# A gated mix of segment attention and a GeGLU block on one core: first loads in 128 KB pieces over two queues, gate and up weights by column halves, a new order

## The chip, the cores and the metric

The kernel runs on one core of a Trainium2 chip. The metric is the device time of one execution in microseconds; the time before is the median of three runs, and one further execution was profiled. Where a time has a place ("at 17.94"), it is counted from the start of the profiled span.

## The reference

With x of 2048 rows by 512 columns (bfloat16), the output is `g * a + (1 - g) * b`, a row at a time, with `g = sigmoid(sum(x * gate_w))`.

- `a` is attention with 32 heads of width 16 in four segments of 512 rows. In each segment: `q = x @ wq`, `k = x @ wk`, `v = x @ wv`; causal softmax attention inside the segment; plus a read of a running memory, `num = phi(q) @ M` over `den = phi(q) . z`, mixed in by a per-head sigmoid of `beta`; then `M` and `z` are increased by `phi(k)^T v` and by the sum of `phi(k)`. `phi(t)` is `t + 1` for positive t and `exp(t)` otherwise. The heads' result goes through `wo`.
- `b = (gelu(x @ w_gate) * (x @ w_up)) @ w_down` with 1792 hidden columns.

## The kernel before

The work is cut into tasks, each a short run of instructions on one engine, numbered by segment s (0 to 3) and a tile index. The task names are used throughout:

- `xtr0`, `xev0`: segment 0's x is loaded row-wise (tile `pt`), transposed on TensorE into `psX`, and copied to `xT` (lines 770 to 779). The digits are the half of the rows and the pair of 128-column blocks. For segments 1 to 3, four transposing DMAs per segment, `ld_x1_0` to `ld_x3_3` (line 343), bring `xT` directly.
- `K`, `Q`, `V`: projections. A K or Q tile is four matmuls of 128x512 (line 443) into one of four PSUM banks; K of segment 0 is made in three parts a, b, c of 256 columns (line 469), where a needs blocks 2 and 3 of the first half of x, b blocks 0 and 1, and c the second half. `Kev`, `Qev`, `Vev` copy the result out on ScalarE or VectorE, and `kpada`, `kpadb` spread K for the score matmuls. A V task is four matmuls of 128x256 or 257 (line 492).
- `st`, `exp`, `msk`, `pv`: score fills into the 2048-column `psX` (line 596), one ScalarE exponential of 1.88 us each (line 602), the causal mask on GpSimd (line 608), and the product with V (line 638). `tp`, `pvp`, `ot` normalise and transpose on VectorE.
- `phk`, `phq`, `mz`, `nd`: phi of k and q, memory write and memory read. `ktr`, `otr`, `vsh` are their DMAs on SyncE's queue (SP).
- `G`, `U`: 14 gate tiles and 14 up tiles per segment, four matmuls each (line 443); `Gev` and `gelu`, `gd` finish the gate, `h` multiplies. `out`, `wo`, `wev`, `oev`, `dma` are the down projection, the output projection, the mix, and the store.
- `warm1`: matmuls on a zero tile at the start (line 377). `betab`, `bexp`, `gq`, `gfull`, `gwtr`, `gwev` prepare the head gates and the row gate.

Nothing is planned while the kernel is built: the string `ORDER` lists every task by name, and the tasks go out on their engines in that order. A suffix after a colon is a bank number for a TensorE task that opens a bank (`G0_1:0`) or the engine for an eviction (`Gev0_1:d` on VectorE, `:a` on ScalarE). Each engine runs its tasks strictly in its order, and the waits between engines follow from what the tasks read and write. Tasks named `ld_` are DMA issues on SP or ScalarE; one with a `wait` list is held on its queue until the named loads have landed, and all that stands behind it on that queue is held too. Before the change, SP issues x0_0, wk0, wq0 (waits for x0_0), wq1 (waits for x0_1), gw, wv (waits for wk0), two transposes of x1 (the first waits for wq0), wg0 (waits for wq1), the two other transposes, beta, wg1 (waits for wv), and after the first `vsh` the weights wu, wo, wd and x2. ScalarE issues wk1 and x0_1.

Of the kernel before, what the change touches and what calls it, by code (L numbers as in the profile page):

```python
# [246 lines left out]
def _build(es, nc, A_x, A_wq, A_wk, A_wv, A_wo, A_beta, B_w_gate, B_w_up, B_w_down, gate_w, out):  # L247
# [216 lines left out]
    def project(s):  # L464
        b, b3 = s % 2, s % R_XT
        k0 = [Slot() for _ in range(4)]
        for nm, kbs, h in (("a", (2, 3), 0), ("b", (0, 1), 0), ("c", (0, 1, 2, 3), 1)) if s == 0 else ():
            for t in range(4):
                one(f"K0_{t}{nm}", PE, len(kbs) * T_MM / 2, [I(lambda e, t=t, i=i, h=h: e.matmul(
                    BK[k0[t].i][:, 256 * h:256 * h + 256], wk[:, i, t * 128:(t + 1) * 128], xT[0][:, i, 256 * h:256 * h + 256],  # L470
                    start=(i == 2 - 2 * h), stop=(i == 1 + 2 * h)), [("xT", 0, i, "h0"), ("wk", i // 2),
                    *([("xT", 0, i)] if h else [])], [bk(k0[t])]) for i in kbs], opens=(nm == "a"))
# [374 lines left out]
warm0 causal1 ld_wk1 ident ld_x0_0 causal0 warm1:0 xtr0_01 consts masks vones0 gwz ld_wk0 ld_x0_1 ld_wq0 xtr0_00  # L847
xev0_01:d K0_2a:1 K0_0a:2 ld_wq1 ld_gw K0_1a:3 xev0_00:d K0_2b xtr0_10 xtr0_11 K0_0b K0_3a:0 K0_3b K0_1b xev0_10:a
xev0_11:d K0_1c Kev0_1:a K0_3c K0_0c K0_2c Kev0_3:a Kev0_0:a Kev0_2:d ld_wv Q0_0:3 Q0_1:0 Qev0_0:a kpadb0_0 kpada0_0
st0_0A gwtr:2 exp0_0A Q0_3:1 kpada0_3 gwev Qev0_1:d V0_3b:3 V0_0b:2 V0_2b:0 Vev0_3b:d ld_x1_0 ld_x1_1 ld_wg0 ld_x1_3  # L850
ld_x1_2 V0_0a:3 Vev0_0b:d Qev0_3:d Vev0_2b:a st0_0B Vev0_0a:a exp0_0B ld_beta ld_wg1 Q0_2:2 V0_2a:0 V0_1a:1 Q1_3:3
Vev0_2a:a Qev0_2:d Qev1_3:d Vev0_1a:a st0_0C kpadb0_3 phka0_0 kpadb0_1 causal kpada0_1 Q1_1:2 Qev1_1:d G0_1:0 V0_3a:1
V0_1b:3 exp0_0C phkb0_0 Vev0_3a:d Gev0_1:d phkc0_0 st0_0D exp0_0D Q1_2:2 G0_2:1 G1_0:0 st0_0E Qev1_2:d Gev1_0:d
kpadb0_2 Vev0_1b:a exp0_0E G0_6:2 G0_0:3 V1_1a:0 betab Gev0_2:d bexp phka0_2 phqa1_2 Gev0_6:d Gev0_0:d vsh0_00 vsh0_01
vsh0_20 vsh0_21 ld_wu1 ktr0_0 ld_wo st0_1A ld_wu0 ld_x2_2 ld_x2_0 ktr0_1 ld_wd0 V1_3a:1 G1_3:2 G0_3:3 msk0_0A msk0_0B
msk0_0C msk0_0D msk0_0E Vev1_3a:d Gev1_3:d Gev0_3:d exp0_1A phkb0_2 Vev1_1a:a st0_1B pv0_0:12 Q1_0:3 G1_2:0 gq tp0_d01
exp0_1B st0_1C exp0_1C Qev1_0:a phkc0_2 tp0_d00 Gev1_2:d K1_0:2 msk0_1B V1_3b:1 K1_1:0 Vev1_3b:d kpada0_2 st0_1D
exp0_1D Kev1_1:d Kev1_0:d pvp0_00 pvp0_01 V1_2a:1 G1_5:3 K1_2:0 Kev1_2:d Gev1_5:a Vev1_2a:d st0_2A G0_5:2 K1_3:3
exp0_2A G0_4:0 Gev0_5:d Gev0_4:d msk0_1C msk0_1A msk0_1D Kev1_3:d kpada1_0 ktr0_2 ktr0_3 pv0_1:12 st0_2B tp0_d11
kpada1_1 tp0_d10 G0_12:0 V1_2b:3 G0_7:2 Vev1_2b:d G0_11:1 G0_8:3 gelu0 gd0_12 gd0_7 G0_10:0 gd0_8 gd0_11 gd0_10  # L860
ld_x2_3 ld_x2_1 G0_13:2 gd0_13 phka1_0 ot0_0 G0_9:3 ld_wd1 G1_1:1 V1_1b:0 mz0_2:2 gd0_9 exp0_2B kpadb1_2 pvp0_10
V1_0b:3 Vev1_1b:d Vev1_0b:d mzacc0_2 U0_5:0 h0_5 mz0_0:3 U0_10:2 st0_2C mzacc0_0 kpadb1_1 h0_10 phka1_2 Gev1_1:d
phkb1_0 G1_6:0 U0_4:3 V1_0a:2 phqa1_0 Vev1_0a:d kpadb1_0 gz0 Gev1_6:d h0_4 exp0_2C st0_2D exp0_2D K2_0:1 G1_4:2 Q2_1:0
Gev1_4:a phkc1_0 Kev2_0:d st0_2E Q2_0:3 U0_13:2 U0_3:1 exp0_2E msk0_2A msk0_2B msk0_2D msk0_2C msk0_2E Qev2_1:d h0_3
h0_13 st0_3A U0_9:0 U0_2:1 K2_1:2 Qev2_0:a phqb1_2 pvp0_11 h0_2 kpada1_2 Kev2_1:d h0_9 exp0_3A st0_3B pv0_2:31 phqb1_0
gr0 exp0_3B U0_7:2 U0_12:0 st0_3C tp0_d21 gz1 ot0_1 tp0_d20 h0_7 go0 U0_11:1 U0_1:3 h0_12 h0_1 kpada2_1 h0_11 U0_6:2
# [76 lines left out]
```

## Time and profile before

| what | value |
|---|---|
| median of three runs | 271.32 us (270.82 to 271.83) |
| profiled execution | 270.53 us |
| its span in the profile | 268.8 us |
| TensorE matmul busy | 257.1 us (96%) |
| VectorE, ScalarE, GpSimd busy | 206.9, 203.0, 95.5 us |
| moved by DMA | 16.48 MB, mean 61 GB/s |
| granted TensorE clock | 1.00 throughout |

A row of TensorE's instructions in order of time gives start, duration, engine (PE, or PEld for the weight load that overlaps), line, operation, tiles, shape and count, and in brackets the idle time before it with what ended it. A matmul's duration contains its pipeline, so a run of four 128x512 matmuls that lasts 1.03 us by its row keeps the engine for four spacings of 0.216, some 0.865 us. The chain that ended last is followed back from the last instruction; each row is a start, a duration, and what the time was spent in. The time between the span and the execution (1.73 us) lies outside the profile.

### The profile page before, as it was taken

The numbers are of one execution on the slowest core, as the hardware profiler recorded it, in microseconds if no ns is written. First come the engines' busy times: TensorE is split into PE (matmuls) and PEld (weight loads), VectorE is DVE, ScalarE is ACT, GpSimd is POOL, SyncE is SP. The second block draws the span as 40 slices with busy tenths as digits, with TensorE's granted clock in tenths as the row PEclk, the third lists the DMA queues.
The fourth block names the chain that finished last, engine by engine and source line by source line (L and its number), as shares of the span: only waits on it lengthen the run. The fifth ranks groups of instructions, "written<-read, shape, count | busy, mean of one in ns | idle before, by whom it ended". The sixth has DMA issues, their size and how long they took to land.

```text
span 268.8 us, 6340 instructions
## 1 busy us (share of the span) xinstructions
PE 257.1 (96%) x2632; PEld 121.4 (45%) x2669; DVE 206.9 (77%) x434; ACT 203.0 (76%) x171; POOL 95.5 (36%) x150
## 2 busy tenths in 40 slices
PE   7989799999999999999999999899999999999995
PEld 4644345543444444444454444445443444444342
DVE  1458898397989707898588998997899659887883
ACT  1668779889689987899878787777788886868712
POOL 6008271027333502442125464145513034254500
PEclk9999999999999999999999999999999999999999
DMA  6881799600000253002063000012301000012012
GB/s 195 246 226 22 188 246 196 176 2 2 2 2 0 57 104 81 1 2 59 0 100 83 0 2 2 0 43 62 61 2 40 0 2 2 0 48 63 12 41 78
DMA packets 30117, 16.48 MB, mean 61 GB/s; under 512 B 20488, under 2 KB 29064, under 8 KB 30088
## 3 DMA queue, kind: packets, MB, share of 16 engines
q1 hardware_dynamic: 29544, 15.55, 24.6%
q10 hardware_dynamic: 544, 0.52, 0.6%
q8 instruction: 21, 0.34, 0.5%
q14 instruction: 8, 0.07, 0.1%
HBM read 8.14 MB, written 2.10 MB: 38 GB/s over the span
## 4 chain that ended last, share of the span: by engine, by line
PE 74%; DVE 12%; DMA 4%; issue 3%; SPq 2%; ACT 2%; POOL 1%; ACTq 0%; DVEq 0%
PE psD L443 38%; PE psD L715 16%; PE psX L596 7%; PE psD L638 4%; PE psD L729 4%; PE psD L492 3%; DMA xT<-in_A_x_dram 2%; DVE gb L700 2%; DMA pt<-in_A_x_dram 2%; SPq L343 1%; POOL pt L608 1%; ACT pt L602 1%; PE psD L540 1%; PE psD L571 1%; DVE kD L481 1%
## 5 line engine op out<-in xcount | busy, mean ns | idle before, releaser
L602 ACT ACTIVATE pt<-psX 128x2048 bf16<-128x2048 f32 x72 | 135.1, 1877 | 39.8 <-PE psX L596 38.0
L608 POOL TENSOR_TENSOR pt<-pt,ctri 128x256 bf16<-128x256 bf16 x128 | 91.5, 721 | 158.6 <-ACT pt L602 139.3
L443 PE MATMUL psD<-xT,wu 128*128 128x512 bf16 x213 | 52.7, 380 | 1.3 <-issue 0.5
L715 PE MATMUL psD<-wd,gb 128*128 128x512 bf16 x217 | 52.8, 380 | 0.9 <-issue 0.6
L443 PE MATMUL psD<-xT,wg 128*128 128x512 bf16 x213 | 51.4, 379 | 2.3 <-DVE gb L437 1.3
L700 DVE TENSOR_TENSOR gb<-psD,gb 128x512 bf16<-128x512 f32 x56 | 37.6, 683 | 9.7 <-PE psD L443 9.5
L443 PEld LDWEIGHTS psD<-xT,wg 128*128 128x128 bf16 x224 | 20.9, 98 | 26.3 <-DVE gb L437 1.5
L715 PEld LDWEIGHTS psD<-wd,gb 128*128 128x128 bf16 x224 | 20.2, 98 | 24.7 <-issue 3.4
L443 PEld LDWEIGHTS psD<-xT,wu 128*128 128x128 bf16 x224 | 20.0, 97 | 23.5 <-issue 2.6
L596 PE MATMUL psX<-qT,kD 32*128 32x192 bf16 (+7 forms) x512 | 28.6, 287 | 0.3 <-DVE kD L481 0.2
L523 DVE STREAM_TRANSPOSE tT<-psD 128x512 f32<-128x512 f32 x32 | 22.0, 703 | 5.1 <-PE psD L638 4.8
L499 DVE CAST vnat<-psD 128x256 bf16<-128x256 f32 x20 | 8.4, 419 | 14.8 <-PE psD L492 14.6
L638 PE MATMUL psD<-pt,vnat 64*17 64x128 bf16 (+7 forms) x512 | 18.9, 283 | 0.1
L492 PE MATMUL psD<-wv,xT 128*128 128x256 bf16 (+1 forms) x128 | 18.5, 273 | 0.5 <-DVE omem L554 0.5
L649 DVE SCALAR_TENSOR_TENSOR ob<-tT,gq,rc 128x256 bf16<-128x256 f32 x32 | 17.7, 552 | 1.1
L638 PE MATMUL psD<-pt,vsh 64*17 64x128 bf16 (+7 forms) x512 | 18.4, 283 | 0.0
L596 PEld LDWEIGHTS psX<-qT,kD 32*128 32x128 bf16 x512 | 8.2, 92 | 22.3 <-issue 7.8
L683 ACT ACTIVATE gb<-psD 128x512 bf16<-128x512 f32 x28 | 15.2, 593 | 3.9 <-PE psD L443 3.9
L437 DVE CAST gb<-psD 128x512 bf16<-128x512 f32 x23 | 15.6, 682 | 2.3 <-PE psD L443 2.3
L443 PE MATMUL psD<-xT,wq 128*128 128x512 bf16 x61 | 15.8, 380 | 1.2 <-DMA xT<-in_A_x_dram 1.0
L729 PE MATMUL psD<-wo,oT 128*128 128x512 bf16 (+1 forms) x65 | 15.5, 366 | 0.4 <-issue 0.3
L492 PEld LDWEIGHTS psD<-wv,xT 128*128 128x128 bf16 x128 | 12.0, 97 | 7.8 <-DVE omem L554 1.0
(83 smaller groups left out, 268.1 us busy)
## 6 DMA issues: line engine op xcount, KB each, us to landing
out_dram<-ost SPq DMA_DIRECT2D x15, 128.0 KB, 1.7
wg<-in_B_w_gate_dram SPq DMA_DIRECT2D x2, 896.0 KB, 5.9
wu<-in_B_w_up_dram SPq DMA_DIRECT2D x2, 896.0 KB, 6.3
wd<-in_B_w_down_dram SPq DMA_DIRECT2D x2, 896.0 KB, 5.9
vsh<-vnat SPq DMA_DIRECT2D x16, 68.0 KB, 2.1
wq<-in_A_wq_dram SPq DMA_DIRECT2D x2, 256.0 KB, 2.6
wv<-in_A_wv_dram SPq DMA_DIRECT2D x1, 512.0 KB, 4.2
wo<-in_A_wo_dram SPq DMA_DIRECT2D x1, 512.0 KB, 4.4
```

The lines of the kernel that those rows point to most:

```text
L437: (DVE, 0.60, [I(lambda e: e.tensor_copy(dst, src()), [bk(sl), *reads], writes)]),
L443: one(name, PE, n * T_MM, [I(lambda e, i=i: e.matmul(BK[sl.i][:, :], lhs(i), rhs(i), start=(i == 0), stop=(i == n - 1)), reads(i), [bk(sl) ...
L492: one(f"V{s}_{m}{'ab'[hf]}", PE, 2 * T_MM, [I(lambda e, i=i, sl=sl, a=a, z=z, xs=xs: e.matmul(BK[sl.i][:, 0:z - a], xs(i), wv[:, i, a:z], ...
L523: one(f"tp{name}", DVE, 0.605, [I(lambda e, sl=sl, ti=ti: e.transpose(tT[ti][:, :], BK[sl.i][:, :]), [bk(sl)], [("tT", ti)])], bias=bias)
L596: ins.append(I(lambda e, t=t, kb=kb, ncol=ncol, c0=c0, g=g: e.matmul(XALL[:, g * 512 + c0:g * 512 + c0 + ncol], kD[b][32 * g:32 * g + 32, ...
L602: one(f"exp{s}_{name}", ACT, 2048 * 0.000833 + 0.05, [I(lambda e: e.activation(pt[slot][:, :, :], xin, ACTF.Exp, scale=ATT_SCALE), [("X",) ...
L608: ins.append(I(lambda e, mv=mv: e.tensor_tensor(mv, mv, cm, ALU.mult), [("pt", slot), ("causal",)], [("pt", slot)]))
L638: ins.append(I(lambda e, kb=kb, slot=slot, c0=c0, n=n, g=g, r0=r0, sl=banks[j], va=va: e.matmul(BK[sl.i][32 * g:32 * g + 17, 64 * kb:512], ...
L649: I(lambda e, ti=ti, ri=ri, t=t, j=j, dst=dst: e.scalar_tensor_tensor(out=dst, in0=t_rows(ti), scalar=gq[:, 2 * t + j:2 * t + j + 1], in1= ...
L700: one(f"h{s}_{ft}", DVE, 0.605, [I(lambda e, sl=sl, gi=gi, f=f: e.tensor_tensor(gb[gi][:, f, :], BK[sl.i][:, :], gb[gi][:, f, :], ALU.mult ...
L715: mm.append(I(lambda e, fb=fb, gi=gi, f=f, q=q, sl=sl: e.matmul(BK[sl.i][:, :], gb[gi][:, f, q], wd[:, fb, :], start=(fb == 0), stop=(fb = ...
L729: one(f"wo{s}_{qt}{sfx}", PE, 4 * T_MM / len(parts), [I(lambda e, kb=kb, q=q, so=so, c=c, w=w: e.matmul(BK[so.i][:, 0:w], oT[:, kb, q], wo ...
```

## The change

- Segment 0's x and the key weights, 512 KB each, were loaded in four pieces of 256 KB. They come now in eight of 128 KB: x by 128-row blocks, wk by 128-row blocks of the weight. SP issues x0_0, wk2, wk0, x0_2, and ScalarE x0_1, wk3, wk1, x0_3.
- The waits of `wq0` and `wq1` follow the new pieces: wq0 waits for x0_1, wq1 for wk3 (before: x0_0 and x0_1, each then half of x).
- The two pieces of the gate weights and of the up weights were halves by input rows (two of four 128-row blocks, all 1792 columns). They are now halves by columns (all four blocks, 896 columns), so tile ft needs the piece ft // 7 alone.
- `warm1` has six matmuls where it had eight.
- The whole order is planned anew: the sequence on every engine, the bank numbers, and which engine takes which eviction.

```diff
+    fhalf = (slice(0, HFT * P), slice(HFT * P, DF))
...
-    ld_xp(0, 0, SP)
-    ld_xp(0, 1, ACT)
-    ld_w("wk0", SP, wk[:, halves[0], :], wsrc(A_wk)[:, halves[0], :], [("wk", 0)], 0.25)
-    ld_w("wk1", ACT, wk[:, halves[1], :], wsrc(A_wk)[:, halves[1], :], [("wk", 1)], 0.25)
+    for eng, i in ((SP, 0), (ACT, 1), (SP, 2), (ACT, 3)):
+        if i == 2:
+            for e2, kb in ((SP, 2), (ACT, 3), (SP, 0), (ACT, 1)):
+                ld_w(f"wk{kb}", e2, wk[:, kb, :], A_wk[kb * P:(kb + 1) * P, :], [("wk", kb)], 0.125)
+        ld_w(f"x0_{i}", eng, pt[stage[0]][:, i, :], A_x[0, i * P:(i + 1) * P, :], [("xs", 0, i)], 0.125)
...
-    ld_w("wq0", SP, wq[:, halves[0], :], wsrc(A_wq)[:, halves[0], :], [("wq", 0)], 0.25, ["x0_0"])
-    ld_w("wq1", SP, wq[:, halves[1], :], wsrc(A_wq)[:, halves[1], :], [("wq", 1)], 0.25, ["x0_1"])
+    ld_w("wq0", SP, wq[:, halves[0], :], wsrc(A_wq)[:, halves[0], :], [("wq", 0)], 0.25, ["x0_1"])
+    ld_w("wq1", SP, wq[:, halves[1], :], wsrc(A_wq)[:, halves[1], :], [("wq", 1)], 0.25, ["wk3"])
...
-    ld_w("wg0", SP, wg[:, halves[0], :], wgr[:, halves[0], :], [("wg", 0)], 0.9, ["wq1"])
+    ld_w("wg0", SP, wg[:, :, fhalf[0]], wgr[:, :, fhalf[0]], [("wg", 0)], 0.9, ["wq1"])
...
-                             [("warm",)], [bk(s0)]) for _ in range(8)], bias=9000.0, opens=True)
+                             [("warm",)], [bk(s0)]) for _ in range(6)], bias=9000.0, opens=True)
...
-                       lambda i: [*xk(s, i), ("wg", i // 2)], 4)
+                       lambda i: [*xk(s, i), ("wg", ft // HFT)], 4)
```

(wg1, wu0, wu1 and the U tiles likewise; K's tiles read `("wk", i)`, and the transposes the two row blocks they use.) The order up to the first product with V, before:

```
warm0 causal1 ld_wk1 ident ld_x0_0 causal0 warm1:0 xtr0_01 consts masks vones0 gwz ld_wk0 ld_x0_1 ld_wq0 xtr0_00
xev0_01:d K0_2a:1 K0_0a:2 ld_wq1 ld_gw K0_1a:3 xev0_00:d K0_2b xtr0_10 xtr0_11 K0_0b K0_3a:0 K0_3b K0_1b xev0_10:a
xev0_11:d K0_1c Kev0_1:a K0_3c K0_0c K0_2c Kev0_3:a Kev0_0:a Kev0_2:d ld_wv Q0_0:3 Q0_1:0 Qev0_0:a kpadb0_0 kpada0_0
st0_0A gwtr:2 exp0_0A Q0_3:1 kpada0_3 gwev Qev0_1:d V0_3b:3 V0_0b:2 V0_2b:0 Vev0_3b:d ld_x1_0 ld_x1_1 ld_wg0 ld_x1_3
ld_x1_2 V0_0a:3 Vev0_0b:d Qev0_3:d Vev0_2b:a st0_0B Vev0_0a:a exp0_0B ld_beta ld_wg1 Q0_2:2 V0_2a:0 V0_1a:1 Q1_3:3
Vev0_2a:a Qev0_2:d Qev1_3:d Vev0_1a:a st0_0C kpadb0_3 phka0_0 kpadb0_1 causal kpada0_1 Q1_1:2 Qev1_1:d G0_1:0 V0_3a:1
V0_1b:3 exp0_0C phkb0_0 Vev0_3a:d Gev0_1:d phkc0_0 st0_0D exp0_0D Q1_2:2 G0_2:1 G1_0:0 st0_0E Qev1_2:d Gev1_0:d
kpadb0_2 Vev0_1b:a exp0_0E G0_6:2 G0_0:3 V1_1a:0 betab Gev0_2:d bexp phka0_2 phqa1_2 Gev0_6:d Gev0_0:d vsh0_00 vsh0_01
vsh0_20 vsh0_21 ld_wu1 ktr0_0 ld_wo st0_1A ld_wu0 ld_x2_2 ld_x2_0 ktr0_1 ld_wd0 V1_3a:1 G1_3:2 G0_3:3 msk0_0A msk0_0B
msk0_0C msk0_0D msk0_0E Vev1_3a:d Gev1_3:d Gev0_3:d exp0_1A phkb0_2 Vev1_1a:a st0_1B pv0_0:12 Q1_0:3 G1_2:0 gq tp0_d01
...
```

and after:

```
warm0 ld_x0_0 ld_x0_1 ld_wk3 ld_wk1 causal0 masks ident consts causal1 warm1:0 xtr0_01 xev0_01:d ld_wk2 vones0 gwz
xtr0_00 xev0_00:d ld_wk0 ld_x0_2 ld_x0_3 ld_wq0 ld_wq1 ld_gw ld_beta ld_wv K0_1a:1 K0_2a:2 K0_0a:3 K0_3a:0 K0_3b
xtr0_10 xtr0_11 K0_2b K0_0b K0_1b xev0_10:d ld_x1_0 ld_x1_3 ld_x1_2 ld_x1_1 xev0_11:d K0_3c Kev0_3:d K0_0c K0_2c
Kev0_0:d kpada0_0 K0_1c Kev0_1:a kpadb0_0 ld_wg0 Q0_0:0 Q0_3:3 Qev0_0:a Kev0_2:a gwtr:1 st0_0A Q0_1:0 gwev phka0_0
Qev0_3:d kpadb0_3 V0_1b:1 Q0_2:2 causal Vev0_1b:d Qev0_1:d exp0_0A st0_0B exp0_0B V0_3b:3 V0_1a:1 Vev0_3b:d Vev0_1a:d
V0_0b:0 V0_2b:3 V0_3a:1 Qev0_2:a Vev0_0b:a Vev0_2b:d kpada0_1 st0_0C exp0_0C V0_0a:3 Q1_1:2 V0_2a:0 phkb0_0 Qev1_1:a
Vev0_0a:d kpadb0_1 Vev0_2a:d betab Vev0_3a:d msk0_0A G0_3:3 st0_0D G1_0:0 G1_3:2 G0_1:1 ld_wg1 vsh0_00 ld_wu1 vsh0_20
vsh0_01 vsh0_21 exp0_0D Gev1_0:a Gev0_3:d kpadb0_2 kpada0_2 Gev1_3:d st0_0E G0_0:3 Q1_2:2 V1_1b:0 phkc0_0 exp0_0E bexp
st0_1A Gev0_1:d Vev1_1b:a phka0_2 gz0 Gev0_0:d V1_3b:1 Qev1_2:d Vev1_3b:d exp0_1A Q1_3:3 msk0_0B msk0_0C msk0_0D
msk0_0E pv0_0:02 tp0_d00 Qev1_3:d phkb0_2 st0_1B exp0_1B msk0_1A msk0_1B tp0_d01 G0_4:1 G0_5:0 Q1_0:3 Gev0_5:a
...
```

The two orders go on for some 60 lines like these; the tail (the last four stores) has the same shape in both.

More of the change, by code (lines that the diff above doesn't have):

```diff
@@ L362, in _build @@
     ld_xt(1, "wq0")
-    ld_w("wg0", SP, wg[:, halves[0], :], wgr[:, halves[0], :], [("wg", 0)], 0.9, ["wq1"])
-    ld_w("wg1", SP, wg[:, halves[1], :], wgr[:, halves[1], :], [("wg", 1)], 0.9, ["wv"])
-    ld_w("wu0", SP, wu[:, halves[0], :], wur[:, halves[0], :], [("wu", 0)], 0.9, ["wg0"])
-    ld_w("wu1", SP, wu[:, halves[1], :], wur[:, halves[1], :], [("wu", 1)], 0.9, ["wg0"])
+    ld_w("wg0", SP, wg[:, :, fhalf[0]], wgr[:, :, fhalf[0]], [("wg", 0)], 0.9, ["wq1"])
+    ld_w("wg1", SP, wg[:, :, fhalf[1]], wgr[:, :, fhalf[1]], [("wg", 1)], 0.9, ["wv"])
+    ld_w("wu0", SP, wu[:, :, fhalf[0]], wur[:, :, fhalf[0]], [("wu", 0)], 0.9, ["wg0"])
+    ld_w("wu1", SP, wu[:, :, fhalf[1]], wur[:, :, fhalf[1]], [("wu", 1)], 0.9, ["wg0"])
     ld_w("wd0", SP, wd[:, 0:HFT, :], wdr[:, 0:HFT, :], [("wd", 0)], 0.9, ["wg1"])
@@ L698, in glu_up @@
             sl = dense(f"U{s}_{ft}", lambda i, c=c: wu[:, i, c], lambda i: xT[s % R_XT][:, i, :],
-                       lambda i: [*xk(s, i), ("wu", i // 2)], 4, wait=[("g", gi, f)])
+                       lambda i: [*xk(s, i), ("wu", ft // HFT)], 4, wait=[("g", gi, f)])
             one(f"h{s}_{ft}", DVE, 0.605, [I(lambda e, sl=sl, gi=gi, f=f: e.tensor_tensor(
@@ L772, in _build @@
                 pt[stage[0]][:, q, kb * 128:(kb + 1) * 128], ident[:, :]),
-                [("xs", 0, h), ("pt", stage[0]), ("ident",)], [("X", j)]) for kb in (2 * p, 2 * p + 1) for q in (2 * h, 2 * h + 1)])
+                [("xs", 0, 2 * h), ("xs", 0, 2 * h + 1), ("pt", stage[0]), ("ident",)], [("X", j)]) for kb in (2 * p, 2 * p + 1) for q in (2 * h, 2 * h + 1)])
             dst = xT[0][:, 2 * p:2 * p + 2, 256 * h:256 * h + 256]
@@ L846 @@
 ORDER = """
[L847 to L866, printed above, removed]
@@ new lines @@
+st0_1A Gev0_1:d Vev1_1b:a phka0_2 gz0 Gev0_0:d V1_3b:1 Qev1_2:d Vev1_3b:d exp0_1A Q1_3:3 msk0_0B msk0_0C msk0_0D
+msk0_0E pv0_0:02 tp0_d00 Qev1_3:d phkb0_2 st0_1B exp0_1B msk0_1A msk0_1B tp0_d01 G0_4:1 G0_5:0 Q1_0:3 Gev0_5:a
+Qev1_0:d kpada0_3 st0_1C K1_3:2 G0_2:0 K1_1:3 exp0_1C gq phkc0_2 st0_1D Kev1_1:d pvp0_00 Gev0_2:a Kev1_3:a exp0_1D
+K1_0:0 G1_2:2 V1_2b:3 Gev0_4:a kpada1_3 Kev1_0:d Gev1_2:d msk0_1D pvp0_01 st0_2A gr0 exp0_2A msk0_1C G0_6:0 Vev1_2b:d
+Gev0_6:d G1_5:1 V1_0b:2 V1_2a:3 Vev1_0b:d Vev1_2a:d Gev1_5:d st0_2B pv0_1:02 ld_wo ktr0_0 tp0_d10 kpada1_0 ktr0_1
@@ new lines @@
+phka1_0 tp0_d11 G0_13:3 G0_8:1 gelu0 gd0_8 ld_x2_2 ld_wu0 ktr0_3 ld_x2_0 ld_wd0 G0_11:0 gd0_11 G0_9:2 G0_12:1 gd0_9
+gd0_12 gd0_13 G0_7:0 ld_wd1 ld_x2_1 ld_x2_3 ktr0_2 gd0_7 G0_10:2 gd0_10 G1_4:1 U0_3:3 U0_13:0 G1_1:2 h0_3 Gev1_4:d
+kpadb1_0 K1_2:3 h0_13 Gev1_1:d gfull phqa1_2 Kev1_2:d exp0_2B st0_2C U0_10:1 mz0_0:0 phkb1_0 exp0_2C U0_8:2 st0_2D
+K2_0:3 h0_10 h0_8 phkc1_0 Kev2_0:d mz0_2:1 U0_4:2 h0_4 mzacc0_2 exp0_2D st0_2E exp0_2E Q2_1:3 V1_3a:2 U0_5:1 mzacc0_0
+pvp0_11 h0_5 Qev2_1:a st0_3A exp0_3A V1_1a:0 U0_2:3 U0_9:1 msk0_2C msk0_2A Vev1_3a:d Vev1_1a:d msk0_2B h0_2 msk0_2D
```

101 lines of the change are left out of this document (52 added, 49 removed).

## The prediction

> **What bounds the kernel now.** I read the page first, then busy time by stretches, TensorE's instructions in order of time, the chain that ended last, and VectorE's in the worst stretch.
>
> ```profile
> PE 257.1 (96%) x2632; PEld 121.4 (45%) x2669; DVE 206.9 (77%) x434; ACT 203.0 (76%) x171; POOL 95.5 (36%) x150
> ```
>
> TensorE bounds the whole: 96% busy; in the page's 40 slices of 6.72 us those under 90% are four of the first five, one in mid-run and the last. By stretches:
>
> ```profile
> 0.00:4.46 4.46, 3.39 (x9) 1.15 (x9) 0.22 (x2) 1.28 (x1) 3.44 (x17) 1.00 0.54 163
> 4.46:16.60 12.14, 11.74 (x101) 8.18 (x102) 5.64 (x15) 7.27 (x11) 0.63 (x7) 1.00 0.96 252
> 16.60:24.50 7.90, 6.94 (x47) 2.90 (x46) 5.39 (x11) 5.63 (x8) 3.98 (x5) 1.00 0.23 88
> 24.50:29.40 4.90, 3.49 (x29) 1.64 (x30) 4.60 (x11) 3.92 (x5) 2.97 (x5) 1.00 0.50 94
> 29.40:260.00 230.60, 225.66 (x2421) 104.83 (x2456) 187.16 (x390) 183.56 (x148) 84.53 (x119) 1.00 0.21 48
> ```
>
> (Columns: stretch, its length, PE, PEld, DVE, ACT, POOL busy, clock, DMA share, GB/s.) From 29.4 to 260 us TensorE idles 4.94 us in 230.6: little to win. The work of 0 to 4.46 is padding (eight warm matmuls). The holes:
>
> ```profile
> 1.07 3.60 PE L377 MATMUL psD<-warm 128*128 128x512 bf16 x8 [1.07 <-POOL warm L373]
> 4.46 0.70 PE L770 MATMUL psX<-ident,pt 128*128 128x128 bf16 x8
> 5.46 1.05 PE L469 MATMUL psD<-xT,wk 128*128 128x256 bf16 x8 [0.30 <-DVE xT L779]
> ...
> 16.60 0.38 PE L443 MATMUL psD<-xT,wq 128*128 128x512 bf16 x1
> 17.94 0.61 PE L443 MATMUL psD<-xT,wq 128*128 128x512 bf16 x2 [0.96 <-DMA xT<-in_A_x_dram]
> ...
> 27.51 0.61 PE L492 MATMUL psD<-wv,xT 128*128 128x256 bf16 x4
> 29.38 1.90 PE L443 MATMUL psD<-xT,wg 128*128 128x512 bf16 x8 [1.25 <-DVE gb L437]
> ```
>
> Hole A, at 16.60: Q1_3 waits for a transposed load of segment 1's x. The chain says why:
>
> ```profile
> 1.33 4.70 DMA pt<-in_A_x_dram
> ...
> 11.73 6.16 DMA xT<-in_A_x_dram
> ```
>
> SP holds wq1 until x0_1 lands (1.33 + 4.70 = 6.03), so gw, wv and the four transposes behind it slip (the first goes out at 7.36); the last transpose goes out at 11.73 behind a 896 KB piece of wg (issued 9.91) and takes 6.16 us where the least is 3.5. Hole B, at 27.95: G1_3 needs the bank of G0_6, whose cast stands last in this VectorE queue:
>
> ```profile
> 25.51 1.22 DVE L744 COPY betab<-omem 32x8 bf16<-32x8 bf16 x4
> 26.76 0.69 DVE L437 CAST gb<-psD 128x512 bf16<-128x512 f32 x1
> 27.49 0.43 DVE L453 TENSOR_SCALAR phk<-kT 128x1024 bf16<-128x1024 bf16 x1
> 27.83 0.89 DVE L453 TENSOR_SCALAR phq<-qT 128x1024 bf16<-128x1024 bf16 x1
> 28.64 1.27 DVE L437 CAST gb<-psD 128x512 bf16<-128x512 f32 x2
> ```
>
> **First loads.** SP issues x0_0, wk2, wk0, x0_2; ACT x0_1, wk3, wk1, x0_3. The first transposes need x0_0 and x0_1. Today SP's packets start at 1.90 us and its first 128 KB are through at 2.74, ACT's start at 2.66 and reach 128 KB at 3.55; landing lags by 0.5 (262 KB on SP at 3.72, landed 4.25). So the pair lands at about 4.05, against 4.25; bounds 3.25 (ACT's queue as early as SP's) and 4.25. The padding, six instead of eight matmuls at 0.427 us spacing, ends at 1.07 + 2.56 = 3.63 and stops mattering (it cost 0.2 now). Transposes start at 4.15 to 4.2; at the cold spacing (0.107; 0.055 from 4.66 on today) four take 0.43, plus 0.35 to the copy, 0.43 the copy: K0 starts near 5.25 against 5.46. Gain **0.2** (0 to 0.8). After 8 + 2 K0 matmuls at 0.109 the second half of x is wanted at 6.35; it lands at about 6.05 as today (the same megabyte).
>
> What rides along: vones0 (0.17) and gwz (0.11) now stand between VectorE's two xT copies and delay the second by 0.3, hidden by eight K0 matmuls (0.87); uncovered it would cost 0.3. `masks` goes ahead of `ident` on GpSimd: ident at 3.1 instead of 2.0, wanted at 4.05. ACT's two extra issues (0.5 each) push its table load (1.28) to 2.9 to 4.2; its first job is near 9.4. gw now waits for gwz (5.55), and behind it on SP stand beta, wv, the four transposes and wg0.
>
> **SP after that.** wq0 waits x0_1 (4.05), wq1 waits wk3 (4.55 instead of 6.05), gw 5.6, beta 6.05 (0.6), wv 6.7, x1 from 7.1 at 1.25 each: last issued 10.8, ended 12.1, with no weight piece ahead. At 3.5 to 4.3 us it lands at 14.3 to 15.1 (17.0 at 6.2). TensorE wants it (Q1_1) after four Q0 tiles (0.865 each), seven V0 tasks (0.435), three score fills (0.33) and gwtr, from K0's end at 9.2: 9.2 + 3.46 + 3.05 + 1.0 + 0.1 = 16.8. Hole A goes: 17.94 - 16.60 - 0.22 = **1.1**, at the bound 6.2 still 0.9.
>
> What is late next: wg0, issued 12.1 instead of 9.91. Pieces of that size took 5.4 to 6.3 (7.5 at worst, wu): 17.5 to 18.4 (19.6). The first gate tile, G0_3, stands one Q and one V task behind Q1_1, at 16.8 + 0.865 + 0.435 = 18.1. I take 0 (to 1.4 lost). Halving by columns lets G tiles below 7 start on wg0 alone; today both row halves must land (20.0), which cost only 0.26 of weight-load wait, so by itself it is worth 0, but without it the new G0_3 would wait for wg1.
>
> **Hole B.** The new order puts betab ahead of the cast of V0_3a, phqa1_2 long after, and gives Gev1_0 to ScalarE. Adding VectorE's list up with today's durations from Vev0_2a's end at 18.8 (V cast 0.43, other casts 0.69, kpad 0.3, phkc 1.37): betab ends 20.0, Vev0_3a 20.45, Gev0_3 21.1, two kpad 21.7, Gev1_3 22.4, phkc0_0 23.7, Gev0_1 24.4, phka and gz 25.0, Gev0_0 25.6, Qev1_2 26.3. TensorE, added up likewise, wants the last three banks at 25.3 (Gev0_1), 25.7 (Gev0_0, for Q1_3) and 26.6 (Qev1_2, for pv0_0): ready, by 0.1 at the least. Hole B with the 0.2 just before it goes: 1.43 + 0.2 = **1.6**. In its place G1_3 needs Qev1_1, which stands on ScalarE behind exp0_0C and phkb0_0: exp0_0B ends 15.8, Qev0_2 and Vev0_0b take 1.2, exp0_0C 1.88, phkb0_0 1.05, Qev1_1 0.6: 20.55 against 20.25, minus **0.3**; and 0.1 for seams.
>
> **The rest of the order.** Same tasks, so the same TensorE work; evictions only change engines (Gev 23/5 to 19/9 VectorE/ScalarE, wev 7/9 to 11/5). Later loads have room: U0_3 comes near 47, wu0 lands near 35. Counting TensorE work between the last matmul of a bank's user and its next user, 22 of 263 reopenings come within 1.2 us before, 30 after. Today the 22 and all else cost 4.94 us, 0.22 each if they were all of it; eight more at that: 1.8 at most, 0 at least, and another plan could also be up to 1.0 better. I take a loss of **0.5**.
>
> Sum: 0.2 + 1.1 + 1.6 - 0.3 - 0.1 - 0.5 = 2.0 gained. Span 268.8 to 266.8; the profiled execution took 270.53 (1.73 around the span): 268.5; the median 271.32 lies 0.79 above it: **269.3**.
>
> **Rivals.**
> - Cold clock. The spacing falls from 0.107 to 0.055 at 4.6 us, 3.5 after the first warm matmul; now TensorE is idle from 3.63 to 4.15, inside that stretch. If the clock then opens one such stretch (3.5) later, at 8.1, K0 from 5.25 on runs at half speed: 1.4 lost, 0.2 more in the transposes: 270.9. For it: nothing before showed such a gap. Against: 0.5 of 3.5 us only. The Trainium skill, "TensorE: Matmul & The Clock Gate", Part 1, states this rule (a window of about 3.4 us must be busy, free-running); the trace agrees on the length, and nothing here shows the threshold.
> - Pieces cost by count. Second pieces landed 1.4 us behind the first (4.25 to 5.6, 4.57 to 6.03). If the spacing is per transfer, not per byte, the fourth lands at 4.05 + 3 x 1.4 = 8.3, xtr0_10 slips by 2.0: 271.3. Against: packets are 1 KB before and after. The skill's "DMA: Bandwidth & Descriptors", Bandwidth, speaks so against the change (batch to 1 MiB or more); its fixed 2 us per transfer is not seen between pieces here.
> - Late wg0 with a slightly worse plan: 1.4 + 0.5 lost: 271.2, no change.
> - Tight banks (slower). Each of the eight extra reopenings waits one VectorE cast (0.68) queued ahead: 5.4 instead of 0.5 lost: **274.2**. It decides for slower from five of eight on (3.4 us). For it: VectorE is 77% busy and hole B is that case; against: the 22 of today mostly cost nothing.
> - The order does not do what it says (x1 still late, hole A only moved): 270.4.
>
> **Chances.** A measurement of this kernel tells 0.5% (1.36 us) from no change. Forecast 0.55, faster; own range 267.9 to 269.9. Cold clock 0.08, pieces 0.06, late wg0 0.08, order 0.05: all within 0.5%, 0.27. Tight banks 0.18, slower. Low end: K0 0.6 earlier and the plan 1.0 better instead of 0.5 worse: 267.2. High end: seven of the eight in the slower case, 273.4, cut to 273.0.
>
> **What would show it.** K0 starting at 5.2 to 5.3; the spacing 0.055 or 0.109 by then; no wait for xT at the first segment 1 tile; wg0 landing by 18.1; pv0_0 near 26.6 against 31.54 (two gate tiles and a fill, 2.06, now come behind it); idle from there to 260 near 5.4. Wrong, if that idle grows by over 3 us.

## The result and the profile after

| | before | after |
|---|---|---|
| median of seven runs each, side by side | 270.58 us (269.97 to 271.83) | 268.98 us (268.64 to 269.33) |
| profiled execution | 270.53 us | 269.33 us |
| its span | 268.8 us | 267.6 us |

The ratio is 0.9936, with a 95% interval of 0.9915 to 0.9957: faster by 1.6 us of medians and by 1.2 us between the two profiled spans. The forecast was 2.0 gained and a time of 269.3 us.

The page of the changed kernel, busy time by engine:

```profile
PE 257.5 (96%) x2629; PEld 121.9 (46%) x2667; DVE 207.1 (77%) x435; ACT 203.5 (76%) x172; POOL 95.2 (36%) x150
```

The same five stretches as before (columns: stretch, its length, PE, PEld, DVE, ACT, POOL busy, clock, DMA share, GB/s):

```profile
0.00:4.46 4.46, 3.40 (x14) 1.50 (x14) 0.19 (x1) 1.28 (x1) 3.19 (x20) 1.00 0.50 156
4.46:16.60 12.14, 11.78 (x93) 7.70 (x93) 6.83 (x22) 5.47 (x6) 1.53 (x4) 1.00 0.80 223
16.60:24.50 7.90, 7.85 (x61) 3.57 (x60) 6.75 (x17) 7.40 (x9) 4.64 (x6) 1.00 0.88 288
24.50:29.40 4.90, 4.69 (x94) 2.55 (x94) 3.33 (x9) 4.71 (x8) 2.37 (x4) 1.00 0.64 165
29.40:260.00 230.60, 225.09 (x2352) 104.28 (x2385) 186.22 (x384) 183.93 (x150) 83.52 (x118) 1.00 0.20 41
```

TensorE's idle time fell from 0.96 to 0.05 us between 16.60 and 24.50 and from 1.41 to 0.21 between 24.50 and 29.40: both holes are shut. The last row needs care. It seems to idle 5.51 us in 230.6, but the run of the old order with three edits, below, holds 2456 matmuls there where before held 2421, and is busy for 229.91:

```profile
29.40:260.00 230.60, 229.91 (x2456) 105.16 (x2456) 187.99 (x391) 183.32 (x147) 83.92 (x119) 1.00 0.22 48
```

The records that before and after lack (37 and 38 matmuls of 128x512 in the whole span, while their weight loads are all there) look like idle time.

TensorE's instructions in order of time:

```profile
1.06 2.74 PE L379 MATMUL psD<-warm 128*128 128x512 bf16 x6 [1.06 <-POOL warm L375]
3.62 1.03 PE L772 MATMUL psX<-ident,pt 128*128 128x128 bf16 x8
4.75 1.98 PE L471 MATMUL psD<-xT,wk 128*128 128x256 bf16 x10
6.95 0.62 PE L772 MATMUL psX<-ident,pt 128*128 128x128 bf16 x8 [0.21 <-DMA pt<-in_A_x_dram]
7.40 2.56 PE L471 MATMUL psD<-xT,wk 128*128 128x256 bf16 x22
...
17.85 0.81 PE L445 MATMUL psD<-xT,wq 128*128 128x512 bf16 x3
18.50 0.60 PE L494 MATMUL psD<-wv,xT 128*128 128x256 bf16 x4
18.94 1.02 PE L445 MATMUL psD<-xT,wg 128*128 128x512 bf16 x4
19.90 0.40 PE L598 MATMUL psX<-qT,kD 32*128 32x320 bf16 x8
20.23 2.76 PE L445 MATMUL psD<-xT,wg 128*128 128x512 bf16 x12
...
27.26 0.39 PE L640 MATMUL psD<-pt,vnat 64*17 64x512 bf16 x4
```

Q1_1 (17.85), G0_3 (18.94) and the twelve matmuls of G1_0, G1_3 and G0_1 (20.23) have no bracket: nothing is waited for. But K0's first ten matmuls take 1.98 us where the same kind took 1.05 for eight before, and the second transposes wait 0.21 for x. The chain that ended last now contains that load, the second half of x, issued at 2.21:

```profile
2.21 4.68 DMA pt<-in_A_x_dram
```

**Where the time went.** Busy sums are spoilt by missing records, so I use the start of single tasks. For each task I take its start in the trace (that of its first weight load, which is never missing) less the TensorE work that its order places ahead of it (each kind of task at its spacing, the warm matmuls left out). The constants of this sum are rough, but they are the same for all kernels, so the differences of this "delay" show where one kernel gains on another:

| delay at the start of | before | after | gained so far |
|---|---|---|---|
| Q0_0, just behind K0 | 4.91 | 5.31 | -0.40 |
| Q1_1, the first tile on segment 1 | 6.46 | 5.61 | 0.85 |
| pv0_0 | 8.35 | 6.13 | 2.22 |
| the last product with wo | 16.96 | 15.77 | 1.19 |

The head lost 0.4, hole A gave 1.25, hole B 1.37, and the rest of the order gave back 1.03. The sum is the 1.2 us between the spans. The border between A and B is good to some 0.1: Q1_1's first weight load in the changed kernel runs 0.11 ahead of its matmul, in the old one it does not, and by the matmuls the two holes gave 1.13 and 1.49.

### The profile page after: what moved, and what is told of

Read it like the earlier page. It is cut to its first block, busy times and chain, and to the rows that moved or that the text cites. A ratio compares the mean times of both kernels' runs of the same rounds, so it can differ in the third digit from the quotient of the medians.

```text
span 267.6 us, 6336 instructions
## 1 busy us (share of the span) xinstructions
PE 257.5 (96%) x2629; PEld 121.9 (46%) x2667; DVE 207.1 (77%) x435; ACT 203.5 (76%) x172; POOL 95.2 (36%) x150
## 4 chain that ended last, share of the span: by engine, by line
PE 77%; DVE 12%; ACT 3%; issue 3%; DMA 3%; SPq 1%; DVEq 0%; ACTq 0%
PE psD L445 40%; PE psD L717 12%; PE psX L598 7%; PE psD L640 5%; PE psD L494 5%; PE psD L731 4%; DMA pt<-in_A_x_dram 2%; DVE oT L656 2%; DVE ob L651 1%; PE psD L573 1%; DVE oT L658 1%; PE psD L542 1%; DVE tT L525 1%; ACT gb L680 1%; DVE gb L439 1%
## 5 line engine op out<-in xcount | busy, mean ns | idle before, releaser
L445 PE MATMUL psD<-xT,wu 128*128 128x512 bf16 x215 | 53.5, 379 | 1.4 <-DVE ost L735 0.4
L702 DVE TENSOR_TENSOR gb<-psD,gb 128x512 bf16<-128x512 f32 x56 | 36.9, 684 | 15.4 <-PE psD L445 15.0
L651 DVE SCALAR_TENSOR_TENSOR ob<-tT,gq,rc 128x256 bf16<-128x256 f32 x32 | 18.1, 566 | 1.1
L494 PE MATMUL psD<-wv,xT 128*128 128x257 bf16 (+1 forms) x128 | 18.6, 273 | 0.1
L445 PE MATMUL psD<-xT,wq 128*128 128x512 bf16 x58 | 15.2, 380 | 0.4 <-issue 0.2
L735 DVE SCALAR_TENSOR_TENSOR ost<-psD,gtok,wds 128x512 bf16<-128x512 f32 (+1 forms) x17 | 12.0, 716 | 4.4 <-PE psD L731 4.2
L640 PEld LDWEIGHTS psD<-pt,vnat 64*17 64x17 bf16 x512 | 11.6, 86 | 7.9 <-issue 3.8
```

The source lines that it names most:

```text
L445: one(name, PE, n * T_MM, [I(lambda e, i=i: e.matmul(BK[sl.i][:, :], lhs(i), rhs(i), start=(i == 0), stop=(i == n - 1)), reads(i), [bk(sl) ...
L494: one(f"V{s}_{m}{'ab'[hf]}", PE, 2 * T_MM, [I(lambda e, i=i, sl=sl, a=a, z=z, xs=xs: e.matmul(BK[sl.i][:, 0:z - a], xs(i), wv[:, i, a:z], ...
L640: ins.append(I(lambda e, kb=kb, slot=slot, c0=c0, n=n, g=g, r0=r0, sl=banks[j], va=va: e.matmul(BK[sl.i][32 * g:32 * g + 17, 64 * kb:512], ...
L651: I(lambda e, ti=ti, ri=ri, t=t, j=j, dst=dst: e.scalar_tensor_tensor(out=dst, in0=t_rows(ti), scalar=gq[:, 2 * t + j:2 * t + j + 1], in1= ...
L702: one(f"h{s}_{ft}", DVE, 0.605, [I(lambda e, sl=sl, gi=gi, f=f: e.tensor_tensor(gb[gi][:, f, :], BK[sl.i][:, :], gb[gi][:, f, :], ALU.mult ...
```

## The experiments: each part alone in the old order

These four ran together; the kernel before took 270.59 us. The first moves three tasks on VectorE and ScalarE, and nothing else:

```diff
 in ORDER
-... V1_1a:0 betab Gev0_2:d bexp phka0_2 phqa1_2 Gev0_6:d Gev0_0:d ...
+... V1_1a:0 Gev0_2:d phka0_2 Gev0_6:d Gev0_0:d betab ...
+    bexp behind exp0_1A, phqa1_2 behind gz0
```

> The kernel before with three tasks moved in its order and nothing else: betab behind Gev0_0, bexp behind exp0_1A, phqa1_2 behind gz0. Theory (hole B is VectorE's queue: G0_6's bank waits behind betab 1.22 and phqa1_2 0.89): G1_3 follows V1_3a without the 1.43 us hole, the span is 1.2 to 1.5 us shorter, about 269.2 against 270.6. Rival (VectorE is simply full there, 77% busy over the run, and the wait reappears at the next bank): within 0.4 us of before, with a wait of like size on pv0_0 or Q1_0.

Measured 269.20 us, ratio 0.9944 (0.9924 to 0.9964). G1_3 stood at 29.38 behind a wait of 1.25; in this run's trace it follows the V task without one:

```profile
28.31 1.89 PE L443 MATMUL psD<-xT,wg 128*128 128x512 bf16 x8
```

Hole B was the queue ahead of G0_6's cast.

The second puts segment 1's transposes first, and keeps the gate weights in halves by rows:

```diff
-... [("wq", 1)], 0.25, ["x0_1"])
+... [("wq", 1)], 0.25, ["wk1"])
 in ORDER: ld_wg0 behind ld_x1_2, the last of the four transposes
```

> The kernel before with wq1 waiting for the second half of wk instead of x0_1, and all four transposes of x1 ahead of wg0; weights still by row halves. Theory (hole A is the late x1): Q1_3 and Q1_1 run without a wait, 1.1 us earlier, but G0_1, due then at 18.4, needs both row halves, and wg1 slips to 19.5 to 21.3: a new wait of 1 to 2.5 us, so the time is 0 to 1 us above before, 270.6 to 271.6. Rival (the four transposes cost nothing to wg1, since the transfers share the same engines): 1.1 us faster, 269.5.

Measured 271.59 us, ratio 1.0055 (1.0028 to 1.0082): slower. The wait for x has gone, and a longer one for the second half of the gate weights has come, while hole B stays:

```profile
PE psD L443 <- DMA wg<-in_B_w_gate_dram: 2.4, 1, 2.4
PE psD L443 <- DVE gb L437: 1.3, 1, 1.3
```

(Waits of TensorE: tile, line, releaser, total us, times, longest.) Nine of its twelve executions lie at 270.9 to 272.5 with a mean granted clock of 0.998 to 1.000, three at 273.0 to 274.4 with 0.994; the profile is of the nine. The third adds the halves by columns to that:

```diff
+    fhalf = (slice(0, HFT * P), slice(HFT * P, DF))
-... wg[:, halves[0], :], wgr[:, halves[0], :] ...   ("wg", i // 2)
+... wg[:, :, fhalf[0]], wgr[:, :, fhalf[0]] ...     ("wg", ft // HFT)
 (wg1, wu0, wu1 likewise)
```

> As the run with SP's order changed, and gate and up weights by column halves. Theory: G0_1 needs wg0 alone (landing 17.4 to 18.0), so hole A closes and nothing takes its place: 1.0 to 1.2 us faster than before, 269.5. Rival (column halves are worth nothing by themselves, as the forecast said of the old order): same as the run with row halves.

Measured 269.48 us, ratio 0.9956 (0.9938 to 0.9973). Columns against rows are worth 2.1 us here (2.0 without the three executions at 0.994), and hole A, thus really removed, 1.1. Hole B is where it was, 1.25 long, in the old place:

```profile
28.87 1.90 PE L444 MATMUL psD<-xT,wg 128*128 128x512 bf16 x8 [1.25 <-DVE gb L438]
```

The fourth joins all three edits, still in the old order and with the old four first pieces:

> The old order with all three small edits: SP's order, column halves, and the three VectorE and ScalarE moves; first loads still in four pieces of 256 KB, eight warm matmuls. Theory (the gain of the changed kernel comes from holes A and B, and its head and the rest of its plan lose): 2.2 to 2.6 us faster than before, 268.2, that is 0.6 to 0.9 below the changed kernel. Rival (the new plan as a whole carries the gain): 269.0 or more.

Measured 268.17 us, ratio 0.9908 (0.9887 to 0.9928), span 266.8. 1.1 and 1.4 add to 2.4. TensorE's longest waits behind the start are

```profile
PE psD L493 <- DVE omem L555: 0.5, 1, 0.5
PE psX L597 <- DVE kD L482: 0.2, 1, 0.2
```

So a few edits to the old order give all that the change gave, and 0.8 us of span more (266.8 against 267.6). Neither the eight pieces nor the new plan is needed for it.

## The experiments: parts of the changed kernel undone

These four ran together; the kernel before took 270.11 us beside them. First, gate and up weights by row halves again, wg1 issued right behind wg0:

```diff
-... wg[:, :, fhalf[0]], wgr[:, :, fhalf[0]] ...     ("wg", ft // HFT)
+... wg[:, halves[0], :], wgr[:, halves[0], :] ...   ("wg", i // 2)
```

> The changed kernel with gate and up weights loaded by row halves again, all else as changed. Theory (the new order rests on the column halves): G0_3, due at 18.9, waits for wg1, which landed at 21.3 in the changed kernel: a wait of 2.0 to 2.5 us named after the load of wg, time 271.0 to 271.5. Rival (column halves are worth nothing by themselves, as forecast for the old order): 269.0, no wait.

Measured 271.27 us, ratio 1.0051 (1.003 to 1.0071), as expected, and with a surprise: the nine executions form two groups, five at 270.4 to 271.3 with a mean granted clock of 1.000, four at 272.2 to 272.6 with 0.994. The profile is of the upper group. The wait for wg1, then three stretches around it, then the gate tiles behind it:

```profile
PE psD L445 <- DMA wg<-in_B_w_gate_dram: 2.1, 1, 2.1
```

```profile
19.20:22.70 3.50, 1.43 (x14) 0.47 (x14) 2.46 (x7) 1.53 (x3) 1.13 (x2) 0.99 0.85 265
22.70:26.10 3.40, 3.40 (x10) 1.23 (x9) 1.25 (x4) 1.99 (x2) 1.33 (x2) 0.51 0.47 122
26.10:28.00 1.90, 1.90 (x16) 0.68 (x15) 1.90 (x4) 0.97 (x1) 0.00 (x0) 1.00 0.63 217
```

```profile
22.20 4.45 PE L445 MATMUL psD<-xT,wg 128*128 128x512 bf16 x12
```

For 3.4 us behind the wait the clock is granted at 0.51, and twelve matmuls take 4.45 us instead of 2.76. A stall of 2.1 us was paid for a second time, with 3.4 x 0.49 = 1.7. The Trainium skill, "TensorE: Matmul & The Clock Gate", Part 1, has the clock fall to half after an idle window of some 3.4 us. The length of the slow stretch agrees; but TensorE worked for 1.43 of the 3.5 us ahead of it, so if these were the window, it need not be idle throughout.

Such a wait does not always cost the clock. In the profile of the old order with x first and row halves the same wait was longer, and the clock stayed:

```profile
22.32 0.61 PE L443 MATMUL psD<-xT,wg 128*128 128x512 bf16 x2 [2.37 <-DMA wg<-in_B_w_gate_dram]
```

```profile
22.00:24.00 2.00, 1.68 (x18) 1.01 (x18) 0.60 (x2) 0.00 (x0) 1.38 (x3) 1.00 0.00 0
24.00:26.00 2.00, 2.00 (x17) 0.90 (x10) 2.00 (x3) 1.82 (x2) 0.00 (x0) 1.00 0.00 0
```

That kernel has the same two groups of mean clock, and none of its three executions at 0.994 was profiled. What decides between the two is open; the length of the wait alone does not.

Second, four 256 KB pieces of x and wk in place of eight:

```diff
-    for eng, i in ((SP, 0), (ACT, 1), (SP, 2), (ACT, 3)):
-        ...
+    ld_xp(0, 0, SP)
+    ld_xp(0, 1, ACT)
+    ld_w("wk0", SP, ...)   # halves, as before the change
+    ld_w("wk1", ACT, ...)
 wq0 waits for x0_0, wq1 for wk1; ld_wk1 ahead of ld_x0_1
```

> The changed kernel with the first x and key weights in four 256 KB pieces again (wq0 behind the first half of x, wq1 behind the half of wk that is used first), order and six warm matmuls kept. Theory (eight pieces start K0 earlier but their second half of x lands at 6.9 instead of 6.0 to 6.3, so K0 ends no earlier): K0 starts at 5.5 to 5.8 instead of 4.75 and ends within 0.3 us of the changed kernel's 9.8; time 268.7 to 269.3, the same. Rival (eight pieces are worth their earlier start): 0.7 to 0.9 slower, 269.8. Second rival (pieces cost by count): 0.5 faster.

Measured 270.27 us, ratio 0.9983 (0.996 to 1.0006), and no single time: five executions lay at 268.3 to 268.5 and seven at 270.2 to 270.9, all with a clock of 1.000. The profile is of the lower group: x lands at 4.17 and 5.99, K0 runs from 5.34 to 9.3. Read by its profile the larger pieces cost nothing; read by the ratio of the medians (0.9983 against 0.9936) they cost 1.3. The runs on the start, below, take this up.

Third, eight warm matmuls where the change has six:

```diff
-... for _ in range(6)] ...
+... for _ in range(8)] ...
```

> The changed kernel with eight warm matmuls instead of six. Theory (the clock opens at a time that the padding does not set: 4.66, 6.30, 6.30, 6.45, 6.97 and 7.07 us in the six profiles so far, five of them with eight matmuls): the first transposes wait until 4.5 instead of 3.6, K0 starts at 5.4 to 5.7, the clock opens anywhere between 4.6 and 7.1, and the time is 0 to 0.5 above the changed kernel. Rival (the gap in the padding kept the clock low in the changed kernel): the spacing is full speed from 4.7 and the time is 0.4 below it.

Measured 269.27 us, ratio 0.9964 (0.9951 to 0.9977), span 266.9: as the changed kernel within the intervals. The profiled execution (268.63) is one of two that lie below the other four (269.24 to 269.37).

Fourth, the three late waits that give back what was gained. TensorE's waits in the changed kernel beyond 29.4 us:

```profile
PE psD L445 <- ACT gb L685: 0.6, 1, 0.6
...
PE psD L445 <- DVE ost L735: 0.4, 1, 0.4
PE psD L731 <- DVE oT L658: 0.4, 1, 0.4
...
PE psD L445 <- DVE tT L525: 0.2, 1, 0.2
```

The first, the second and the last are meant: G2_12 at 124.89, U3_12 at 240.78 and U3_4 at 205.18. ScalarE's and TensorE's rows at the first:

```profile
119.86 1.28 ACT L680 ACT_TABLE_LOAD   x1 [1.52 <-DVE gb L439]
121.15 3.19 ACT L680 ACTIVATE gb<-gb 128x3584 bf16<-128x3584 bf16 x1
124.25 2.04 ACT L685 ACTIVATE gb<-psD 128x512 bf16<-128x512 f32 x4
```

```profile
124.89 1.47 PE L445 MATMUL psD<-xT,wg 128*128 128x512 bf16 x6 [0.59 <-ACT gb L685]
```

The gelu of 3.19 us waits 1.52 for the last gate eviction, which stands on VectorE; what stands behind the gelu, an eviction among it, comes late. The edits give that eviction to ScalarE, put `go3` behind the eviction that U3_12 waits for, and the spreads of K's last tile behind the transpose that U3_4 waits for:

```diff
-Gev2_3:d                                  +Gev2_3:a
-ndp3_1 go3 oev2_3                         +ndp3_1 oev2_3 go3
-kpada3_3 kpadb3_3 ot2_0 pvp2_20 tp2_d31   +ot2_0 pvp2_20 tp2_d31 kpada3_3 kpadb3_3
```

> The changed kernel with three small moves in the later part of its order: Gev2_3 on ScalarE instead of VectorE, go3 behind oev2_3, kpada3_3 and kpadb3_3 behind tp2_d31. Theory (the new plan gives back about 1.1 us after pv0_0 through single waits, at G2_12, U3_4 and U3_12, whose releasers stand behind other work on VectorE or ScalarE): these three waits (0.6, 0.2 to 0.3 and 0.4) shrink, 0.8 to 1.2 us faster, 267.9. Rival (the engines are as full as before and the waits move to the next bank): within 0.3 of 269.0.

Measured 267.92 us, ratio 0.9924 (0.9912 to 0.9937), span 266.2, the shortest of the profiles. G2_12 no longer has a break ahead of it, but the wait for `ost` turned into one of nearly the same size:

```profile
122.20 3.99 PE L445 MATMUL psD<-xT,wg 128*128 128x512 bf16 x17
```

```profile
240.84 1.04 PE L445 MATMUL psD<-xT,wu 128*128 128x512 bf16 x4 [0.31 <-DVE omem L556]
```

By the delays, from pv0_0 to pv3_3 the three edits gain 0.76 (8.45 against 9.21): 0.61 at G2_12, 0.23 at U3_4, and nothing at U3_12. The wait for `oT` (0.4, at an output product of the tail, 259.76) follows neither order: it is there in the profiles of the changed kernel, of that with eight warm matmuls and of the two last runs below, and absent in this one and in four others of the new order. It looks like a close race that falls now one way and now the other; that is not shown.

## The experiments: the start

These four ran together; the kernel before took 270.60 us.

```diff
 four 256 KB pieces, as above
-... for _ in range(6)] ...
+... for _ in range(8)] ...
```

> The changed kernel with four 256 KB pieces of first x and wk (as in the run before with four pieces, whose executions fell into two groups, 268.3 to 268.5 and 270.2 to 270.9) and eight warm matmuls instead of six, so the padding lasts until 4.49 and reaches the first transposes at about 4.2 without a gap. Theory (the idle time between the padding and the first transposes lets the clock open late in some executions, and those make the upper group): the upper group goes, all executions at 268.3 to 268.8. Rival (the upper group has another cause, such as the order of the pieces' landing): two groups about 2 us apart again, median at 268.5 or 270.5 by luck.

Four 256 KB pieces with eight warm matmuls: 268.89 us (268.56 to 269.00), ratio 0.9934 (0.992 to 0.9948). The upper group is not seen in these five executions.

```diff
 the changed kernel's eight pieces
-... for _ in range(6)] ...
+... for _ in range(4)] ...
```

> The changed kernel with four warm matmuls instead of six: the padding ends at 2.8 to 3.6, the gap ahead of the first transposes grows from about 0.5 to 1.3 us. Theory (the length of the idle stretch decides when the clock opens): the clock opens after 7 us in most executions, K0 and the first Q tiles run cold, 1 to 2 us slower than the changed kernel: 270 to 271. Rival (the time at which it opens does not hang on the padding once some has run): as the changed kernel, 268.6 to 269.4.

Eight 128 KB pieces with four warm matmuls: 269.79 us (268.84 to 270.42), ratio 0.9968 (0.9954 to 0.9983). TensorE's rows, with four warm matmuls and then for the run just above:

```profile
1.06 1.89 PE L379 MATMUL psD<-warm 128*128 128x512 bf16 x4 [1.06 <-POOL warm L375]
3.75 1.01 PE L772 MATMUL psX<-ident,pt 128*128 128x128 bf16 x8 [0.80 <-DMA pt<-in_A_x_dram]
4.85 2.32 PE L471 MATMUL psD<-xT,wk 128*128 128x256 bf16 x10
6.96 1.06 PE L772 MATMUL psX<-ident,pt 128*128 128x128 bf16 x8
```

```profile
4.61 1.04 PE L771 MATMUL psX<-ident,pt 128*128 128x128 bf16 x8
5.73 1.38 PE L470 MATMUL psD<-xT,wk 128*128 128x256 bf16 x10
6.95 0.61 PE L771 MATMUL psX<-ident,pt 128*128 128x128 bf16 x8
```

With four, even the second eight transposes, at 6.96, run at the long spacing (1.06 for eight instead of 0.61). K0 starts 0.9 sooner and ends later.

The last two join edits shown above: the three late evictions and eight warm matmuls, with eight pieces,

> The changed kernel with the three late evictions put right (G2_3's eviction on ScalarE, go3 behind oev2_3, the two spreads of the last segment's K tile 3 behind tp2_d31) and eight warm matmuls. Theory (the two edits lie at opposite ends and add: 1.1 from the three evictions, 0 to 0.4 from a warmer start): 267.4 to 267.9. Rival (what the head gains is lost at the next wait): 267.9, as without the padding.

268.19 us, ratio 0.9906 (0.9891 to 0.9922).

and with four pieces.

> The three late evictions put right, four 256 KB pieces in place of eight of 128 KB, and eight warm matmuls. Theory (the second half of x lands by 6.0 with larger pieces, against 6.9 with the eight, so K0 needs no wait; the eight pieces bring nothing): 267.2 to 267.8, no more than 0.3 from the run with eight pieces. Rival (eight pieces are worth the 0.2 of the forecast or more): 0.2 to 0.6 above the run with eight pieces.

268.23 us, ratio 0.9912 (0.9895 to 0.9928). Eight pieces against four, all else alike: 268.19 to 268.23, no difference that these runs can tell. With the three edits against without, four pieces and eight warm matmuls in both: 268.23 to 268.89, or 0.66, close to the 0.75 that these two profiles give from pv0_0 to pv3_3.

**What the start hangs on.** In each profile the start-to-start time of matmuls falls by half at some moment (0.213 to 0.109 for 256 columns). The granted clock of the stretches does not show this: it reads 1.00 in the changed kernel's first row, 0.00 to 4.46, where the spacing is still the long one. The table gives the moment, to about 0.1 us. Beside it stands the delay at Q0_0, which sums up the whole head:

| kernel | pieces | warm matmuls | spacing halves at | delay at Q0_0 |
|---|---|---|---|---|
| changed, 8 warm | 8 | 8 | 4.0 | 4.62 |
| three edits | 8 | 6 | 4.1 | 5.11 |
| before | 4 | 8 | 4.66 | 4.91 |
| changed, 4 pieces (lower group) | 4 | 6 | 4.7 | 4.80 |
| changed, row halves | 8 | 6 | 5.55 | 5.05 |
| three edits, 8 warm | 8 | 8 | 5.2 to 5.6 | 5.34 |
| changed, 4 pieces, 8 warm | 4 | 8 | 6.0 | 5.30 |
| changed | 8 | 6 | 6.25 | 5.31 |
| old order, all three edits | 4 | 8 | 6.25 | 5.47 |
| old order, x first, columns | 4 | 8 | 6.45 | 5.54 |
| three edits, 4 pieces, 8 warm | 4 | 8 | 6.45 | 5.55 |
| old order, x first, rows | 4 | 8 | 6.97 | 5.73 |
| old order, VectorE edit | 4 | 8 | 7.07 | 5.81 |
| changed, 4 warm | 8 | 4 | 8.75 | 6.17 |

The delay follows the third number far more than the first two: 0.3 to 0.4 us for each us that the spacing halves later (one profile of each kernel). The row of the three edits lies off this line, and there the second transposes wait 0.47 us for x. With six or eight warm matmuls that moment lies anywhere from 4.0 to 7.1, a spread of some 3 us among executions with like starts; with eight alone it is the same. With four, the one profile has it at 8.75. The Trainium skill, "TensorE: Matmul & The Clock Gate", Part 1, calls the window of some 3.4 us free-running. A spread of about one window is what that gives, and the traces agree. The 500 ns to either side that the same part of the Trainium skill names is exceeded three times over. That the upper group of the run with four pieces and six warm matmuls halves its spacing one such stretch later still would fit (that kernel has a gap of 0.42 us between padding and transposes, which eight warm matmuls close), but no execution of that group was profiled: it stays open.

## Why the prediction was right, and where its terms were off

- **Hole A, 1.1 forecast, 1.25 measured** (delay from Q0_0 to Q1_1: 1.55 before, 0.30 after; 1.13 by the matmuls' starts). Segment 1's last transpose landed at 14.35, 3.0 after its issue (forecast 14.3 to 15.1). Alone in the old order it gave 1.1.
- **wg0 by 18.1:** it landed at 18.01, 5.4 after its issue, and G0_3 did not wait. The rival of a late wg0 fell.
- **Column halves, "worth 0 by itself":** the second half of that sentence mattered. Once segment 1's x goes first, rows instead of columns cost 2.1 us in the old order and 2.0 in the new one (271.27 against 269.27, the run with eight warm matmuls beside it; 1.3 in the five executions that kept the clock). The term is not zero but the other half of hole A's price.
- **Hole B, 1.6 less 0.3 and 0.1 forecast, 1.37 measured** (1.49 by the matmuls' starts; 1.4 alone in the old order). The sum came near, its parts not all. The wait of 0.3 for Qev1_1 never came: ScalarE was done at 20.62 (forecast 20.55), but G1_3, behind G1_0, was not wanted until 20.23 + 0.86 = 21.1 (forecast 20.25), as TensorE itself was late from the head. VectorE's queue ended as added up: Qev1_2 at 26.54 (forecast 26.3). pv0_0 came at 27.26, not 26.6: the 0.66 is the head again, 0.6 of it K0's end (9.8 instead of 9.2).
- **First loads, 0.2 gain forecast, 0.4 lost in this pair of profiles.** This step failed. Its parts had been added wrongly: 4.15 to 4.2 and 0.43, 0.35, 0.43 give 5.36 to 5.41 for K0's start, not 5.25, and so a gain of 0.1 at most. K0 started at 4.75, sooner than either, since x's first half landed at 3.58 (forecast 4.05). But the spacing did not halve at 4.66, as I had read from the one profile there was; it did at 6.25. And x's second half came at 6.90 (forecast 6.05), 4.7 after its issue, so the early start ran into a wait. The cold-clock rival foresaw a late halving, but at 8.1 and by idle time from 3.63 to 4.15 that was not there: the transposes follow the padding at 3.62 without a break. A break of 0.80 us (four warm matmuls) went with 8.75 in one profile, yet at equal padding the moment wandered over some 3 us, and the profile before had an early one. Four and eight pieces measure the same, so the pieces are worth neither the 0.2 nor the 2.0 lost of the rival that counts them. That the Trainium skill, "DMA: Bandwidth & Descriptors", Bandwidth, advises larger batches did not decide here.
- **The rest of the order, 0.5 lost forecast, 1.03 measured.** The sign was right. The working was not: the price of 0.22 for a tight reopening came from 4.94 us of idle time that was mostly missing records. What the new order lost were single late evictions (0.61 at G2_12, 0.23 at U3_4, 0.4 at U3_12) and the tail's race; they add to more than 1.03, since the old order has a late wait of its own (0.5 for `omem`). The slower rival, eight waits of one cast each, fell: there was no such row.
- **The level:** of the gain of 2.0, 1.2 came between the spans and 1.6 between the medians. The median of before itself came out at 270.58 instead of 271.32, so the forecast of 269.3 was met by 268.98 with an error of the gain (0.4) and one of the level (0.74) that partly cancelled. That much of the hit was luck; the two holes, which carry the gain, were not.
- **Two slips that change nothing:** of before's first five slices three, not four, lie under 90%, and the slow end adds up to about 273.5, not 273.4.

## What to carry to other kernels

Order the transfers of the first 20 us by the moment each is wanted, and cut a weight along the dimension that its first consumer runs through: moving x ahead of the weights lost 1.0 us with row halves and gained 1.1 with column halves. A wait on a bank is mended by a few words in the order of the engine that frees it; here three small edits gave more than a new plan, which brought its own late evictions. Do not judge a change to the first few microseconds by one profile: look first at when the matmul spacing halves in it, since the granted clock does not show it there.

The runs point to the changed order with its three late evictions mended (0.9906 with eight warm matmuls, 0.9924 with six) and to the old order with the three edits (0.9908), all below the changed kernel's 0.9936, though their intervals overlap with its.
